# Landmark sums, spreads, squares and loads placed differently in a Nyström attention + MLP kernel

## The chip, the cores and the metric

The kernel runs on one core of a Trainium2 chip. The metric is the device time of one execution in microseconds (us). A core has five engines that run side by side, each with its own queue in program order: TensorE (PE in the profile; its weight loads are listed as PEld), VectorE (DVE), ScalarE (ACT), GpSimd (POOL) and SyncE (SP), whose queue issues all of this kernel's DMAs. Engines wait for each other through semaphores. An engine that waits holds up everything behind it in its queue.

## The reference

q, k and v have 8 batches, 8 heads, 576 rows and 64 columns. The first half is Nyström attention with 32 landmarks; each landmark is the mean of 18 neighbouring rows of q or of k. The second half is a layer norm and an MLP with 2048 hidden units, with a residual:

```
q_lm = q.reshape(B, H, 32, 18, D).mean(axis=3);  k_lm likewise
A, Bm, C = softmax(q k_lm^T), softmax(q_lm k_lm^T), softmax(q_lm k^T)    # each scaled by 1/8
Z = Bm^T / (norm1(Bm) * norminf(Bm));  6 times: Z = 2 Z - Z Bm Z
x = A Z C v                                # (8, 576, 512)
out = x + relu(layernorm(x) * g @ w1) @ w2 # w1 512x2048, w2 2048x512
```

All matmuls run in fp16 with fp32 sums; inputs and output are fp32.

## The kernel before

**The MLP is the bulk of the work.** The 4608 rows of x make 36 blocks of 128 rows; four blocks are a group, so there are nine groups. The generator `mlp` (L825) yields after nearly every matmul of 512 columns. For a group it makes 64 `psh` matmuls (hidden units, evicted by ScalarE into `hT` with a Relu after every fourth) and 64 `pso` matmuls (output; 16 for a block, then one VectorE instruction `ot` that scales with `rstd` and adds x, and two stores). `fill(n)` (L897) takes n steps of this generator, so that n matmuls are put between two pieces of the attention. All order on TensorE, VectorE, ScalarE and GpSimd is that of the program, since every call goes through `keep_in_program_order`.

**Batches 0 and 1** are handled by `attention` (L314) and written out by hand up to L990. **Batches 2 to 7** are handled in sets: set 0 is batch 2, set 1 is batches 3 and 4, set 2 is batches 5 and 6, set 3 is batch 7. A batch has two units of four heads.

**A set is prepared** by a `Coming` object (L508), in three kinds of steps:

- a load (L540): 576 KB of q, k or v into a staging tile `stg`, of which there are six. Loads, stores and DMA transposes all go through SP's queue.
- a cast (L547) by GpSimd, to the fp16 tile `nat` for q or k (eight tiles), to `natv` for v. For a q whose unit number in the set is at least `first_by_pool`, GpSimd also adds up rows in four tensor_tensor instructions, the tiles `asum`, `asum`, `asum` and `s16` (named s in the profile). I call these a q's sums.
- a job: `turn` (L575) is a VectorE transpose of `nat` into `xT`; where GpSimd has made the sums, it also transposes them (`sT`) and adds two halves into `part`, which I call "sT and add". `add_up` (L589) is the other way to `part`: two VectorE tensor_reduce instructions. `spread` (L599) is two TensorE matmuls `psl` on the finished `part` of two units and a copy `lm` from PSUM, after which the scores can be taken.

The jobs of two units stand in the order turn k, add_up k, turn k, add_up k, turn q (add_up q), turn q (add_up q), spread; in a set of four units the first spread comes after the third k pair of jobs and the second at the end.

**A set's attention** is the generator `attention2` (L656). Its steps are: scores of k for each pair of units (`psb`, `psec`, exps on ScalarE, transposes `ecT` on VectorE); the gram and the product with v (`psse`, `pscv`); six iterations (`psn` on TensorE, `st` on VectorE) with the scores of q (`psea`, `ea`) in the first ones; `zc` (`pszc`, then `zcbd` on VectorE); and five row steps per batch (L478: two `psy` matmuls, a reciprocal and `xblk` on VectorE). A set of one batch has 14 steps, a set of two has 21. After each step come some fills, then `settle`, then perhaps a square, then `prepare` for the set after (one cast with its loads, and a job).

**A finished block** calls `block_done` (L742). From group 2 on, GpSimd makes `negm` (minus the mean) and `xn`, SP issues the DMA transpose `xnT`, and ScalarE squares the deviations (`junk`); every fourth block, `deviations` gives `rstd`. `settle` (L738) puts out what is in the list `later`; `a_square` (L978) puts out one item of the list `squares`.

**PSUM**: `psh`, `pso`, `psl` and the transposes `psxt` share three buffers (pool psM); the scores, `pscv` and `psy` share two (ps2).

Of the kernel before, what the change touches and what calls it, by code (L numbers as in the profile page):

```python
# [9 lines left out]
FP16 = mybir.dt.float16  # L10
# [6 lines left out]
P = 128  # L17
# [3 lines left out]
def kernel(  # L21
# [12 lines left out]
    B, H, S, D = q.shape  # L34
# [4 lines left out]
    LM = 32  # L39
# [12 lines left out]
        name=nc.get_next_instruction_name(), act_func_set_id=6, ins=[], outs=[]))  # L52
# [16 lines left out]
    dve, pool, scalar = Ordered(nc.vector), Ordered(nc.gpsimd), Ordered(nc.scalar)  # L69
    act = scalar.activation  # L70

    def MM(o, l, r, rb=0, cb=0, start=True, stop=True, skip=False):
        keep(nc.tensor.matmul(o, l, r, start=start, stop=stop, tile_position=(rb, cb),  # L73
                              skip_group_check=(skip or cb != 0)))
# [88 lines left out]
    for half in range(2):  # L163
        for e in range(2):
            sl = ds(64 * e + 32 * half, 32)
            nc.gpsimd.tensor_copy(
                out=spread16[sl, half, e, :, :],
                in_=ident16[sl, sl][:, None, :].broadcast_to([LM, 2, LM]))
# [23 lines left out]
    for u in range(U):  # L192
        for nm in ("q", "k"):
            cast_qk(0, u, nm, dve)
        if u == 0:

            dve.tensor_copy(out=bones[:], in_=mask4[:, :, None].broadcast_to([P, 4, 32]))
            for i, t in enumerate(zcbd_buf):
                dve.tensor_copy(out=t[:, ds(0 if i % 2 == 0 else 4 * D, 4)],
                                in_=(mask4[:] if i < 2 else heads_of[i % 2]))  # L200
# [43 lines left out]
    asm = ctx.enter_context(tc.tile_pool(name="asm", bufs=2))  # L244
# [263 lines left out]
    class Coming:  # L508
# [38 lines left out]
        def cast(self, i):  # L547
            nm, w = self.parts[i]
            b, u = self.units[w]
            stg = self.stg.pop(i)  # L550
            if nm == "v":
                natv_of[b] = natv_buf[b % NV]
                pool.tensor_copy(
                    out=natv_of[b][:, u, :, :, 0:D].rearrange("p j r d -> p r j d"), in_=stg[:])
                return
            t = nat.tile([P, 2, NJ, D], FP16, name="nat", tag="nat")
            pool.tensor_copy(out=t[:], in_=stg[:])
            self.n16[i] = t
            if nm == "q" and w >= self.first_by_pool:
                s = asum.tile([P, 2, 4, D], FP32, name="asum", tag="asum")  # L560
                s16 = asm.tile([P, 2, D], FP16, name="s16", tag="s16")
                self.sums[i] = s16
                for o, x, y in ((s[:], t[:, :, 0:4, :], t[:, :, 4:8, :]),
                                (s[:, :, 0:2, :], s[:, :, 0:2, :], s[:, :, 2:4, :]),
                                (s[:, :, 0, :], s[:, :, 0, :], s[:, :, 1, :]),
                                (s16[:], s[:, :, 0, :], t[:, :, 8, :])):
                    with nc.allow_low_precision("sums are rounded once, to fp16"):
                        pool.tensor_tensor(out=o, in0=x, in1=y, op=ALU.add)
# [6 lines left out]
        def turn(self, i):  # L575
            nm, w = self.parts[i]
            t = aprep.tile([P, 2, NJ, LM, 2], FP16, name="xT", tag="xT" + nm, bufs=5 if nm == "q" else 4)
            dve.transpose(t[:].rearrange("p r j t x -> p (r j t x)").bitcast(UINT32),
                          self.n16.pop(i)[:].rearrange("p r j d -> p (r j d)").bitcast(UINT32))
            self.xT[nm, w] = t  # L580
            if i in self.sums:
                s = asm.tile([P, 2, LM // 2, 2, 2], FP16, name="sT", tag="sT")
                dve.transpose(s[:].rearrange("p r l a x -> p (r l a x)").bitcast(UINT32),
                              self.sums.pop(i)[:].rearrange("p r d -> p (r d)").bitcast(UINT32))
                dve.tensor_tensor(out=self.part_of(nm, w), in0=s[:, :, :, 0, :], in1=s[:, :, :, 1, :],
                                  op=ALU.add)
# [12 lines left out]
        def spread(self, y):  # L599
            part = self.part.pop(y)  # L600
            psl = psM.tile([P, 2, 8, LM], FP32, name="psl", tag="pm")
            for half in range(2):
                MM(psl[:, half, :, :].rearrange("p k c -> p (k c)"),
                   spread16[:, half, :, :, :].rearrange("p e a w -> p (e a w)"),
                   part[:].rearrange("p n w r l x -> p (n w r l x)"))
            lm = asm.tile([P, 8, 2, LM], FP16, name="lm", tag="lm", bufs=3)
            dve.tensor_copy(out=lm[:].rearrange("p k h c -> p h k c"), in_=psl[:])
            for i, nm in enumerate(("q", "k")):
                for x in range(2):
                    self.lm[nm, 2 * y + x] = lm[:, ds(4 * i + 2 * x, 2), :, :].rearrange(  # L610
                        "p r h (l x) -> p r (h l) x", x=2)
# [124 lines left out]
    later, squares, negms = [], [], {}  # L736

    def settle():  # L738
        while later:
            later.pop(0)()  # L740

    def block_done(j):  # L742
        g, u = divmod(j, 4)
        if g == 0:
            mean_of(j, dve)
            center(j, scalar if u % 2 == 0 else dve)
        elif g == 1:
            mean_of(j, dve)
            later.append(lambda: center(j, scalar))
        else:  # L750
            later.append(lambda: mean_of(j, pool))
            later.append(lambda: center(j, pool) if g <= mlp_at[0] + 1
                         else uncentered.setdefault(g, []).append(j))
        (squares if g <= 1 else later).append(lambda: square(j))
        if u == 3:
            if g == 1:
                later.append(lambda: ln_ready.add(1))
            (squares if g <= 1 else later).append(lambda: deviations(g))

    def mean_of(j, engine):  # L760
        negms[j] = mstat.tile([P, 1], FP32, name="negm", tag="negm", bufs=16)
        engine.tensor_scalar(out=negms[j][:], in0=rowsum.pop(j)[:], scalar1=-1.0 / DM,
                             scalar2=0.0, op0=ALU.mult, op1=ALU.add)
# [18 lines left out]
    def square(j):  # L782
        g, u = divmod(j, 4)
        if u == 0:
            variances[g] = mstat.tile([P, 4], FP32, name="var", tag="var")
        junk = mxn.tile([P, DM], FP16, name="junk", tag="junk", bufs=1)
        act(junk[:], x_blk[j][:], AF.Square, bias=negms[j][:],
            accum_out=variances[g][:, u:u + 1])

    def deviations(g):  # L790
        lnv = mstat.tile([P, 4], FP32, name="lnv", tag="lnv")
        act(lnv[:], variances.pop(g)[:], AF.Ln, bias=eps_ln[:], scale=1.0 / DM)
        rstds[g] = mstat.tile([P, 4], FP32, name="rstd", tag="rstd")
        act(rstds[g][:], lnv[:], AF.Exp, scale=-0.5)
        ln_ready.add(g)
# [101 lines left out]
    def fill(n):  # L897
        for _ in range(n):
            if not next(stream, False):
                return  # L900
# [56 lines left out]
    cast_v(1)  # L957
    fetch_w2()

    sets = [Coming((2,), 1), Coming((3, 4), 2), Coming((5, 6)), Coming((7,))]  # L960

    def prepare(c, casts, jobs):
        for _ in range(casts):
            if c.casts:
                c.next_cast()
                if not c.loads and c is not sets[-1]:
                    sets[sets.index(c) + 1].next_load()
                else:
                    c.next_load()
        for _ in range(jobs):  # L970
            c.next_job()

# [5 lines left out]
    def a_square():  # L978
        if squares:
            squares.pop(0)()  # L980

    n = 0
    for what in a1:
        fill(fills[what])
        settle()
        if what in ("iteration", "product"):
            a_square()
        if what in ("product", "zc", "rows"):
            n += 1
            prepare(sets[0], 1, 1 if n > 3 else 0)  # L990
    for _ in range(2):
        prepare(sets[0], 1, 1)
        fill(6)

    counts = [[9, 20] + 6 * [6] + [7] + 4 * [7] + [10]]
    counts += [[8, 12, 18, 18, 10, 10, 8, 8, 8, 8, 8] + 10 * [7]]
    counts += [[12, 14, 20, 20, 12, 12, 12, 10, 10, 10, 10] + 10 * [10]]
    counts += [[15, 18] + 6 * [12] + [12] + 5 * [12]]
    for c, after, count in zip(sets, sets[1:] + [None], counts):
        while c.jobs:  # L1000
            prepare(c, 1, 1)
            fill(3)
        for step, _ in enumerate(attention2(c.bs, c)):
            fill(count[step])
            settle()
            if step >= 2:
                a_square()
            if after:
                prepare(after, 1, 1)
    for _ in stream:  # L1010
        pass

# [29 lines left out]
```

## Time and profile before

| | |
|---|---|
| median of five runs | 329.97 us (329.29 to 331.67) |
| profiled execution, its own time | 329.8 us |
| its span, first to last instruction | 328.1 us |
| granted TensorE clock, mean | 0.995 of full speed |
| TensorE, weight loads | 310.9 us, 156.1 us |
| VectorE, ScalarE, GpSimd busy | 151.8, 151.1, 121.6 us |
| moved by DMA | 50.32 MB, 153 GB/s on average |

How to read the lines that follow. The page gives each engine's busy time, then the span in 40 slices of 8.2 us with a digit for tenths of busy time (9 is 90% or more); PEclk is the clock granted to TensorE in tenths. A line of waits says which engine waited, for whom, and the total, the count and the longest in us. A line of the timeline has the start in us, the duration, the engine, the line of the helper (L67 and L73 are the helpers that keep the order), the operation, the tiles as out<-in, and the shapes; in square brackets stands idle time in front of it and what ended that. A line of a tile's statistics has the count and the least, the median and the largest duration in ns.

### The profile page before, as it was taken

The page shows a single profiled execution, that of the slowest core. Times are in us where ns is not written, and L with a number is a line of the kernel's source. Part 1 is how long each engine was busy: PE and PEld are TensorE (multiplying, and loading weights), DVE is VectorE, ACT ScalarE, POOL GpSimd, SP SyncE. Part 2 cuts the span into 40 slices and gives each one's busy share as a digit, 9 for nine tenths or more (in the row PEclk, how much of TensorE's full clock was granted, in tenths as well). Part 3 has the DMA queues.
Part 4 walks back from the last instruction along what each step waited for, and adds up shares of the span by engine and source line. Part 5 has one row for each costly group of instructions (what it writes and reads, how often), then busy time and mean ns, then how long its engine had stood idle before and what let it go on. Part 6 is the DMA issues. An engine that isn't in the chain of part 4 may idle for free.

```text
span 328.1 us, 7899 instructions
## 1 busy us (share of the span) xinstructions
PE 310.9 (95%) x3248; PEld 156.1 (48%) x3248; DVE 151.8 (46%) x398; ACT 151.1 (46%) x295; POOL 121.6 (37%) x186
## 2 busy tenths in 40 slices
PE   7889999599989999989999999999999999999994
PEld 6568654244534444434544444444444444444443
DVE  3666249868987556955455345431243110010012
ACT  3376843349532670469322573663058216305600
POOL 4489777864799280449700020500011200000000
PEclk9999999799999999999999999999999999999999
DMA  7999999958997795870023012420241124032023
GB/s 274 394 387 388 386 388 233 388 146 254 319 253 247 200 271 155 252 133 21 2 66 81 21 32 64 82 50 2 64 108 23 32 66 94 2 78 51 2 56 72
DMA packets 38700, 50.32 MB, mean 153 GB/s; under 512 B 17540, under 2 KB 17800, under 8 KB 38664
## 3 DMA queue, kind: packets, MB, share of 16 engines
q1 hardware_dynamic: 38664, 49.82, 52.7%
q8 instruction: 25, 0.41, 0.5%
q14 instruction: 11, 0.09, 0.1%
HBM read 36.70 MB, written 9.44 MB: 141 GB/s over the span
## 4 chain that ended last, share of the span: by engine, by line
PE 82%; DVE 12%; DMA 3%; issue 1%; SPq 0%; DVEq 0%
PE psh L73 39%; PE pso L73 31%; DVE part L67 3%; DVE xblk L67 2%; DMA stg<-in_k_dram 2%; PE psn L73 2%; PE psy L73 2%; DVE xT L67 2%; PE pscv L73 2%; DVE ot L67 1%; PE psec L73 1%; DMA xnT<-xn 1%; PE pst L77 1%; PE psea L73 1%; DVE rcpd L67 1%
## 5 line engine op out<-in xcount | busy, mean ns | idle before, releaser
L73 PE MATMUL psh<-xnT,w 128*128 128x512 f16 (+1 forms) x640 | 135.2, 358 | 1.2 <-DMA xnT<-xn 1.2
L73 PE MATMUL pso<-w,hT 128*128 128x512 f16 (+1 forms) x592 | 133.9, 375 | 0.7 <-issue 0.7
L67 ACT ACTIVATE hT<-psh 128x512 f16<-128x512 f32 x144 | 84.9, 599 | 89.1 <-PE psh L73 88.8
L73 PEld LDWEIGHTS <-w 128*128 128x128 f16 x640 | 59.1, 98 | 59.0 <-issue 2.9
L73 PEld LDWEIGHTS <-hT 128*128 128x128 f16 x592 | 56.3, 98 | 59.8 <-issue 3.2
L67 DVE SCALAR_TENSOR_TENSOR ot<-pso,rstd,xblk 128x512 f32<-128x512 f32 (+1 forms) x37 | 27.2, 734 | 76.5 <-PE pso L73 76.3
L67 POOL TENSOR_SCALAR negm<-rowsum 128x1 f32<-128x1 f32 x28 | 5.4, 191 | 97.2 <-DVE xblk L67 93.7
L67 ACT ACTIVATE junk<-xblk,negm 128x512 f16<-128x512 f32 x36 | 26.0, 723 | 25.7 <-POOL negm L67 25.6
L67 POOL CAST nat<-stg 128x1152 f16<-128x1152 f32 x28 | 31.8, 1146 | 12.7 <-DMA stg<-in_q_dram 9.9
L67 DVE SCALAR_TENSOR_TENSOR xblk<-psy,rcpd 128x512 f32<-128x512 f32 (+1 forms) x40 | 27.6, 691 | 2.2
L67 DVE SCALAR_TENSOR_TENSOR st<-st,psn 128x128 f16<-128x128 f16 (+2 forms) x36 | 11.4, 317 | 33.5 <-PE psn L73 33.4
L67 POOL CAST natv<-stg 128x1152 f16<-128x1152 f32 x16 | 18.5, 1162 | 7.8 <-DMA stg<-in_v_dram 7.8
L67 DVE TENSOR_REDUCE part<-xT 128x32 f16<-128x576 f16 x30 | 21.0, 743 | 0.0
L67 POOL TENSOR_SCALAR xn<-xblk,negm 128x512 f16<-128x512 f32 x28 | 19.3, 694 | 4.8 <-DMA xnT<-xn 3.7
L67 DVE RECIPROCAL rcpd<-psy 128x8 f32<-128x8 f32 (+1 forms) x40 | 8.1, 203 | 24.0 <-PE psy L73 23.8
L67 DVE STREAM_TRANSPOSE xT<-nat 128x576 uint32<-128x576 uint32 x24 | 18.4, 766 | 0.0
L73 PE MATMUL psy<-zcbd,ea 128*128 128x260 f16 (+1 forms) x80 | 15.7, 276 | 0.9 <-DVE zcbd L67 0.8
L73 PEld LDWEIGHTS <-st 32*32 32x32 f16 x448 | 5.7, 89 | 15.1 <-issue 10.4
L73 PEld LDWEIGHTS <-ea 128*128 128x128 f16 (+1 forms) x80 | 7.3, 100 | 10.4 <-issue 2.2
L67 ACT ACTIVATE ea<-psea 128x576 f16<-128x576 f32 x12 | 7.2, 649 | 10.7 <-PE psea L73 10.7
L67 ACT ACTIVATE ec<-psec 128x576 f16<-128x576 f32 x12 | 8.9, 815 | 6.8 <-PE psec L73 6.8
L67 POOL TENSOR_TENSOR asum<-asum 128x256 f32<-128x256 f32 (+1 forms) x18 | 10.7, 593 | 1.4
(101 smaller groups left out, 208.1 us busy)
## 6 DMA issues: line engine op xcount, KB each, us to landing
stg<-in_q_dram SPq DMA_DIRECT2D x16, 576.0 KB, 7.5
stg<-in_k_dram SPq DMA_DIRECT2D x16, 576.0 KB, 7.9
out_dram<-ot SPq DMA_DIRECT2D x70, 128.0 KB, 2.3
wstg<-in_moe_w_ch_dram SPq DMA_DIRECT2D x16, 512.0 KB, 6.9
stg<-in_v_dram SPq DMA_DIRECT2D x10, 576.0 KB, 7.3
stg<-in_v_dram SPq DMA_DIRECT2D x12, 288.0 KB, 8.6
xnT<-xn SPq DMA_TRANSPOSE x28, 2.5
out_dram<-ot SPq DMA_DIRECT2D x4, 64.0 KB, 1.9
```

Source lines behind the costliest of these rows:

```text
L67: return lambda *args, **kw: keep(getattr(self.engine, op)(*args, **kw))
L73: keep(nc.tensor.matmul(o, l, r, start=start, stop=stop, tile_position=(rb, cb), skip_group_check=(skip or cb != 0)))
L77: keep(nc.tensor.matmul(o, i_, idn, is_transpose=True, tile_position=(0, 0)))
```

## The change

It changes where work stands and who does it, and no matmul:

- `first_by_pool` becomes 0 for set 0 (was 1) and 1 for set 1 (was 2): one more q in each has its sums made by GpSimd, and VectorE does sT and add for it instead of add_up. `s16` gets four buffers (was two), `sT` one (was two).
- The copy `lm` of the six spreads goes from VectorE to ScalarE.
- Squares and deviations of all groups go to the list `squares`; one item is put out per step, from step 0 of a set.
- `prepare` casts a q or k only while fewer than eight `nat` tiles wait for their turn, and after a cast it issues loads until three staged tiles wait for their casts, over all sets (before: one load per cast, so six).
- Each step of a set has its own number of fills and says whether it carries a job. Jobs that are left when a set begins are followed by 8 fills each (5 in set 1; before: 3). Set 0's spread has 16 more fills ahead of it.

```diff
-                s16 = asm.tile([P, 2, D], FP16, name="s16", tag="s16")
+                s16 = asm.tile([P, 2, D], FP16, name="s16", tag="s16", bufs=4)
...
-                s = asm.tile([P, 2, LM // 2, 2, 2], FP16, name="sT", tag="sT")
+                s = asm.tile([P, 2, LM // 2, 2, 2], FP16, name="sT", tag="sT", bufs=1)
...
-            dve.tensor_copy(out=lm[:].rearrange("p k h c -> p h k c"), in_=psl[:])
+            scalar.copy(lm[:].rearrange("p k h c -> p h k c"), psl[:])
...
-        (squares if g <= 1 else later).append(lambda: square(j))
+        squares.append(lambda: square(j))
         if u == 3:
             if g == 1:
                 later.append(lambda: ln_ready.add(1))
-            (squares if g <= 1 else later).append(lambda: deviations(g))
+            squares.append(lambda: deviations(g))
...
-    sets = [Coming((2,), 1), Coming((3, 4), 2), Coming((5, 6)), Coming((7,))]
+    sets = [Coming((2,)), Coming((3, 4), 1), Coming((5, 6)), Coming((7,))]
...
-            if c.casts:
+            if c.casts and (c.parts[c.casts[0]][0] == "v" or len(c.n16) < 8):
                 c.next_cast()
-                if not c.loads and c is not sets[-1]:
-                    sets[sets.index(c) + 1].next_load()
-                else:
-                    c.next_load()
+                while sum(len(x.stg) for x in sets) < (3):
+                    left = [x for x in sets if x.loads]
+                    if not left:
+                        break
+                    left[0].next_load()
...
-    for _ in range(2):
+    while len(sets[0].jobs) > 1:
         prepare(sets[0], 1, 1)
         fill(6)
-
-    counts = [[9, 20] + 6 * [6] + [7] + 4 * [7] + [10]]
-    counts += [[8, 12, 18, 18, 10, 10, 8, 8, 8, 8, 8] + 10 * [7]]
-    counts += [[12, 14, 20, 20, 12, 12, 12, 10, 10, 10, 10] + 10 * [10]]
-    counts += [[15, 18] + 6 * [12] + [12] + 5 * [12]]
-    for c, after, count in zip(sets, sets[1:] + [None], counts):
+    fill(16)
+
+    steps = [[(10, 0), (12, 1)] + 6 * [(6, 1)] + [(8, 1)] + 5 * [(6, 0)]]
+    steps += [[(6, 0), (8, 0), (12, 0), (12, 0), (6, 0), (6, 0), (5, 0), (5, 0), (5, 0), (5, 0), (8, 0)] + 3 * [(6, 0)] + 7 * [(7, 1)]]
+    steps += [[(12, 0), (14, 1), (16, 1), (16, 1)] + 6 * [(9, 1)] + [(10, 1)] + 10 * [(8, 1)]]
+    steps += [[(15, 0), (18, 0)] + 6 * [(12, 0)] + [(12, 0)] + 5 * [(12, 0)]]
+    for c, after, plan in zip(sets, sets[1:] + [None], steps):
         while c.jobs:
             prepare(c, 1, 1)
-            fill(3)
-        for step, _ in enumerate(attention2(c.bs, c)):
-            fill(count[step])
+            fill(5 if c is sets[1] else 8)
+        for (count, jobs), _ in zip(plan, attention2(c.bs, c)):
+            fill(count)
             settle()
-            if step >= 2:
-                a_square()
+            a_square()
             if after:
-                prepare(after, 1, 1)
+                prepare(after, 1, jobs)
+    settle()
+    while squares:
+        a_square()
     for _ in stream:
         pass
```

## The prediction

> **What bounds the kernel now.** I read the page first: engine sums, then the 40 slices.
>
> ```profile
> PE 310.9 (95%) x3248; PEld 156.1 (48%) x3248; DVE 151.8 (46%) x398; ACT 151.1 (46%) x295; POOL 121.6 (37%) x186
> PE   7889999599989999989999999999999999999994
> PEclk9999999799999999999999999999999999999999
> ```
>
> TensorE is busy 95% of 328.1 us; no other engine reaches half. The change removes no matmul, so only TensorE's idle time, and a lower clock, can be won. Slice 7 (57 to 66 us) has the one deep hole and the one clock drop. Next, who made TensorE wait (total, times, longest):
>
> ```profile
> PE psl L73 <- DVE part L67: 6.4, 3, 4.3
> PE psh L73 <- DMA xnT<-xn: 1.2, 1, 1.2
> PE psy L73 <- DVE zcbd L67: 0.8, 2, 0.5
> ```
>
> psl is the spread matmul of a set; it needs VectorE's last landmark sum. The timeline gives its three waits: 4.27 us at 61.44, 1.40 at 95.38, 0.73 at 135.69. psh waited 1.24 us at 142.08 for a DMA transpose. One of the two zcbd waits, 0.26 us at 129.28, lies where the change acts. The hole in windows (span, busy by engine, clock, DMA):
>
> ```profile
> 56.80:61.40 4.60, 0.37 (x2) 0.10 (x1) 4.52 (x9) 1.29 (x3) 4.31 (x7) 1.00 1.05 394
> 61.40:62.60 1.20, 1.16 (x5) 0.39 (x4) 0.74 (x2) 0.00 (x0) 1.07 (x1) 0.82 1.05 396
> 62.60:63.80 1.20, 1.20 (x50) 0.61 (x49) 1.13 (x4) 0.21 (x1) 1.03 (x1) 0.50 1.05 404
> 63.80:65.20 1.40, 1.40 (x15) 0.84 (x8) 0.78 (x3) 1.29 (x2) 0.42 (x2) 0.50 1.06 374
> 65.20:66.90 1.70, 1.70 (x24) 0.68 (x21) 1.18 (x3) 0.68 (x2) 1.41 (x2) 0.89 0.93 293
> ```
>
> VectorE is busy 4.52 of 4.60 us while TensorE stands; then TensorE runs at half clock. Lost to the clock: 0.18 x 1.2 + 0.50 x 1.2 + 0.50 x 1.4 + 0.11 x 1.7 = 1.7 us. VectorE's timeline shows what it worked on:
>
> ```profile
> 57.46 0.77 DVE L67 STREAM_TRANSPOSE xT<-nat 128x576 uint32<-128x576 uint32 x1
> 58.26 1.41 DVE L67 TENSOR_REDUCE part<-xT 128x32 f16<-128x576 f16 x2
> 59.59 0.77 DVE L67 STREAM_TRANSPOSE xT<-nat 128x576 uint32<-128x576 uint32 x1
> 60.28 0.20 DVE L67 STREAM_TRANSPOSE sT<-s 128x64 uint32<-128x64 uint32 x1
> 60.52 0.87 DVE L67 TENSOR_TENSOR part<-sT 128x64 f16<-128x64 f16 x1
> 61.86 0.69 DVE L67 CAST lm<-psl 128x512 f16<-128x512 f32 x1 [0.47 <-PE psl L73]
> ```
>
> From start to start: turn 0.70, add_up 1.33, sT 0.24, an ot 0.66 (56.80 to 57.46), a row with its reciprocal 0.85 (133.00 to 133.85). A 512-column matmul takes 0.216 (13.81 us for 64 in the chain), a psy pair, a psl pair or a block's four psxt 0.22 each.
>
> **Part by part.** *Set 0's spread.* Ahead of psl the change puts 28 fills instead of 18: nine pso and one psxt more, 9 x 0.216 + 0.22 = 2.16 us. TensorE was there at 61.44 - 4.27 = 57.17, now at 59.3. On VectorE q of unit 0 loses add_up (1.33) and gains sT and add (0.43). From 57.46: turn, sT, add, turn, sT, add = 2.26, so 59.7. But ot2, now ahead of psl, may own the PSUM buffer that psl takes (three serve pso, psh, psxt and psl): + 0.66. And the add:
>
> ```profile
> L67 DVE TENSOR_TENSOR part<-sT x9: 192/193/868, 60.5 to 174.1; 128x64 f16<-128x64 f16 x9
> ```
>
> The 868 ns one began at 60.52 and ended at 61.39, as GpSimd's cast of 60.20 to 61.34 ended. The Trainium skill, "SBUF — State Buffer", section on the two sides of the memory, speaks against the change here: a VectorE operation with two SBUF inputs and a GpSimd operation lock each other out for a whole instruction. The change makes two more such adds, and two more runs of GpSimd sums beside them. By the row's median an add costs 0.19; by the rule up to the rest of a GpSimd instruction (a cast or first sum, 1.15). The trace has both, so 0.19 to 0.87 each. Ready: 59.7 to 61.7. I take one locked add and the ot, 61.0: the wait falls from 4.27 to 1.7 (0.4 to 2.4). Gain 2.6.
>
> *The clock.* A wait of 1.40 us at 95.38 cost no clock, one of 4.27 did. By these rows alone a wait of 1.7 could go either way: 0 to 1.7 us. The skill's "TensorE: Matmul & The Clock Gate", Part 1, puts the fall to half rate after about 3.4 us of idleness; 1.7 is well under. I take the whole 1.7. After psl, eight fills instead of three cover lm (psb waited about 0.3): gain 0.3.
>
> *lm on ScalarE.* The six casts cost VectorE 685 ns each. The nearest ScalarE row, a copy of 512 columns from PSUM (xnT), takes 581. It queues behind squares (0.72 + 0.19), each of which waits for GpSimd's negm, and hT evictions queue behind it. At every spread 1.1 us or more of fills stand between; cost 0, and 0.6 where that cover is gone.
>
> *Set 1's spread* (wait 1.40). Only eight of its 15 jobs go into set 0's steps, none into the rows; seven follow with five fills each. From the last psy of set 0: VectorE ends its row at 1.4, then two add_ups, two ot, three turns, two sT and adds = 2.66 + 1.32 + 2.10 + 0.86 = 6.9, so 8.3; TensorE has 6 + 30 fills, psy and psl, 7.8 + 0.44 = 8.2. Wait 0.1, with both adds locked 1.5; I take 0.5. Gain 0.9.
>
> *Set 2.* zcbd has no job ahead of it: gain 0.26. The second spread leaves the rows for the seven jobs behind them, with 48 fills (10.4 us) for some 6 us of VectorE work: gain 0.73. The last seven rows are the price: rows 7 x 0.85, jobs 7.0 and two ot 1.3 make 14.3 us of VectorE, against TensorE's 7 x (7 x 0.216 + 0.22) = 12.1. It falls 2.2 behind; psy waits only for the row two before, which allows 2 x 1.73 - 1.4 = 2.1. Cost 0 to 1.5; I take 0.
>
> *psh of group 3* (wait 1.24). Between xn of block 15 and its first use stood 19 fills and three rows, 4.8 us; now 30 fills and five, 7.6. Gain 1.24.
>
> *Fewer fills in set 1's attention.* Step 0 has 6 fills (1.3 us) before psec of the second pair, which needs two ec evictions (0.74 start to start, 0.23 after psec): wait 0.45. The gram then waits for the exp behind them and the softmax: 0.45. The second psea after 6 fills waits for two ea (0.65 each): 0.2. An iteration (psn, st 0.42) fits in 5 fills. Cost 1.1, between 0 and 2.
>
> *Squares and negm.* One list item per step, in ScalarE's order. A square may come one step later; its cover is that step's fills, and no group's rstd is wanted within 3 us. Cost 0.
>
> *GpSimd and the load queue.* Two more q sums, 1.157 + 0.730 + 0.457 + 0.427 = 2.77 us each. Four s16 buffers cover a GpSimd that runs ahead. SP is in order:
>
> ```profile
> 70.07 1.11 SPq L802 DMA_DIRECT2D out_dram<-ot  x2
> 71.28 2.29 SPq L780 DMA_TRANSPOSE xnT<-xn  x1
> 73.66 0.52 SPq L82 DMA_DIRECT2D stg<-in_q_dram  x1
> ```
>
> ```profile
> 77.89 1.14 POOL L67 CAST nat<-stg 128x1152 f16<-128x1152 f32 x1 [4.52 <-DMA stg<-in_q_dram]
> ```
>
> The load behind ot3's store and xnT of block 8 was issued 4.4 us after ot3 (69.29) and used at 77.89. With three loads ahead instead of six, that place falls to unit (3,1)'s q, three casts earlier. ot3 will be near 64.4, so its cast starts near 73 and its sums end near 76.9. VectorE wants them at step 7, near 77.6: margin 0.7, and behind that turn stand st, zcbd and the rows. From there GpSimd has two k casts, two q with sums (3.95 each), three v casts and three negm and xn (2.06 a pair): xn of block 11 at 93.2, landing at 95.7 with the median 2.5 us. TensorE starts group 2's psh near 95.6. In the trace that transpose took 7.4 (issued 90.57) among the loads; now at most three are ahead. Cost 0 to 5; I take 0.5, near the median.
>
> **The sum.** Gains 2.6 + 1.7 + 0.3 + 0.9 + 0.26 + 0.73 + 1.24 = 7.7; costs 1.1 + 0.5 = 1.6; net 6.1. The profiled execution took 329.8 us with a span of 328.1, the median is 329.97: they differ by less than the sum's error. Forecast 329.97 - 6.1 = 323.9.
>
> **Rivals.** *All waits go.* 4.27 + 1.7 + 0.3 + 1.40 + 0.26 + 0.73 + 1.24 = 9.9 and no cost: 320.1. For it: TensorE's 95%; against it: the short fills of set 1.
> *The lock eats the relief.* The adds in sets 0 and 1 and in set 2's rows all wait for GpSimd: 0.7 + 1.0 + 1.5 more, 327.1. For it: three of nine adds were lengthened in the trace; against it: six were not.
> *The change doesn't shorten the queue.* The transpose of block 11 takes 7.4 again: group 2 waits 5.0 instead of 0.5, and the clock falls once (1.7): 323.9 + 4.5 + 1.7 = 330.1, no change.
> *Slower: GpSimd late in set 0.* If two loads, not one, are held for 4.5 us, q of (3,1) is 9 us late against a margin of 0.7: VectorE stops in step 7, st and zcbd with it, TensorE stands 8.3 us and the clock falls: 323.9 + 8.3 + 1.7 = 333.9. It decides from about 6 us of lateness. For it: GpSimd waited 4.52 once; against it: between stores and xnT there is one such place in the set.
>
> **Chances.** A measurement can tell about 0.5%, 1.65 us: no change is 328.3 to 331.6. Forecast (321.8 to 326) 0.50, all waits go 0.17, lock 0.15, queue 0.10, slower 0.08. So faster 0.82, same 0.10, slower 0.08. The range 319.7 to 329.5 leaves out the slower case, half of the queue's and a little at the lower end.
>
> **What would show it.** Right: psl's waits total 2 to 3 us with none over 3.4, slice 7 of the clock at 9, no psh wait at group 3, VectorE's CAST lm gone and six ScalarE copies instead. Wrong: a psh wait for xnT at group 2, VectorE waiting for GpSimd's s or nat in set 0's iterations, psy waiting for xblk in set 1's rows, or lm waiting behind a square.

## The result, and the profile after

The changed kernel takes 329.37 us (median of 43 runs, 327.48 to 334.09), the kernel before 330.16 in the same comparisons (80 runs, 328.27 to 331.88). The ratio is 0.9974, 95% interval 0.9962 to 0.9987: 0.8 us faster where the forecast was 6.1. Medians and ranges here and below are of all executions, while the ratios leave out the few that are over 1.5% above the fastest of their kernel. The profiled execution took 329.3 us with a span of 327.6 and a mean granted clock of 0.993.

The page's engine sums and slices:

```profile
PE 311.5 (95%) x3248; PEld 156.8 (48%) x3248; DVE 146.3 (45%) x392; ACT 154.2 (47%) x301; POOL 126.9 (39%) x194
PE   8789999999976969999999999999999999999994
PEclk9999999999997999999999999999999999999999
```

The work moved as planned: VectorE lost 5.5 us, ScalarE gained 3.1, GpSimd 5.3. The hole and the clock drop of slice 7 are gone. But there are new holes in slices 11, 12 and 14, and the clock drops in slice 12 (98 to 106 us). TensorE's waits (total, times, longest) say for whom:

```profile
PE psh L73 <- DMA xnT<-xn: 2.8, 1, 2.8
PE psn L73 <- issue: 2.6, 1, 2.6
PE psl L73 <- ACT lm L67: 1.8, 1, 1.8
...
PE psl L73 <- DVE part L67: 0.6, 1, 0.6
PE psy L73 <- DVE zcbd L67: 0.5, 1, 0.5
```

psl's 6.4 us of waiting for VectorE shrank to 0.6. Three waits that were not in the profile before stand above it: group 2's psh for the transpose of block 11, set 1's psl for the copy lm (now ScalarE's), and a pause of TensorE that no engine and no data DMA released ("issue").

The timeline shows how the first spread got its gain, on VectorE and TensorE (start, duration; idle time before in brackets):

```profile
57.56 0.77 DVE L67 STREAM_TRANSPOSE xT<-nat 128x576 uint32<-128x576 uint32 x1
58.25 0.20 DVE L67 STREAM_TRANSPOSE sT<-s 128x64 uint32<-128x64 uint32 x1
58.49 0.44 DVE L67 TENSOR_TENSOR part<-sT 128x64 f16<-128x64 f16 x1
...
59.78 0.26 DVE L67 TENSOR_TENSOR part<-sT 128x64 f16<-128x64 f16 x1
...
60.09 0.39 PE L73 MATMUL psl<-part,spread 128*128 128x256 f16 x2 [0.64 <-DVE part L67]
```

The tensor_reduce pair of 1.41 us has gone from between the turns, and psl starts at 60.09 instead of 61.44.

And it shows how the loss of set 1 came about. The lines are of SP's queue, GpSimd, ScalarE and TensorE, in order of time:

```profile
57.67 9.08 SPq L802 DMA_DIRECT2D out_dram<-ot  x6
66.85 2.02 SPq L780 DMA_TRANSPOSE xnT<-xn  x1
68.92 0.56 SPq L82 DMA_DIRECT2D stg<-in_q_dram  x1
...
73.42 1.15 POOL L67 CAST nat<-stg 128x1152 f16<-128x1152 f32 x1 [9.14 <-DMA stg<-in_q_dram]
...
91.55 0.57 SPq L82 DMA_DIRECT2D stg<-in_k_dram  x1
...
93.56 0.57 SPq L82 DMA_DIRECT2D stg<-in_k_dram  x1
...
93.65 0.70 POOL L67 TENSOR_SCALAR xn<-xblk,negm 128x512 f16<-128x512 f32 x1
...
94.23 1.18 SPq L802 DMA_DIRECT2D out_dram<-ot  x2
...
95.42 0.19 POOL L67 TENSOR_SCALAR negm<-rowsum 128x1 f32<-128x1 f32 x1
95.50 1.33 SPq L780 DMA_TRANSPOSE xnT<-xn  x1
95.65 0.72 ACT L67 ACTIVATE junk<-xblk,negm 128x512 f16<-128x512 f32 x1 [0.67 <-POOL negm L67]
...
96.37 0.56 ACT L67 CAST lm<-psl 128x512 f16<-128x512 f32 x1
...
96.98 0.38 PE L73 MATMUL psl<-part,spread 128*128 128x256 f16 x2 [1.85 <-ACT lm L67]
...
100.81 0.59 PE L73 MATMUL psh<-xnT,w 128*128 128x512 f16 x2 [2.80 <-DMA xnT<-xn]
```

The load of unit (3,1)'s q (68.92) stands in SP's queue behind stores (57.67) and the transpose of block 8 (66.85); GpSimd stood still 9.14 us for it. From there to 97.5 us GpSimd works without a gap in which it could win this back, and two things hang on it. First, xn of block 11 ends at 94.35; SP issues its transpose at 95.50, after the store of 94.23, and psh starts 5.3 us after that. Second, ScalarE has in its queue the square of block 12, which waits for GpSimd's negm, and behind it the copy lm of one spread, whose PSUM the next psl has to have. The windows that follow (span, busy time of PE, PEld, DVE, ACT, POOL, granted clock, DMA share, GB/s) show the price:

```profile
96.50:100.80 4.30, 1.03 (x5) 0.48 (x5) 0.75 (x1) 1.02 (x2) 2.14 (x2) 1.00 1.07 234
100.80:103.00 2.20, 2.19 (x52) 0.92 (x52) 0.00 (x0) 0.36 (x1) 0.00 (x0) 0.61 0.99 373
103.00:106.00 3.00, 3.00 (x56) 1.15 (x55) 1.06 (x3) 2.48 (x6) 2.37 (x3) 0.71 1.17 229
```

TensorE worked 1.03 of 4.30 us, and then lost 0.39 x 2.2 + 0.29 x 3.0 = 1.7 us to the lower clock: as much as the change had won back in set 0.

**The balance.** Won against the profile before: set 0's psl 4.27 - 0.64 = 3.6, its clock 1.7, set 2's psl 0.73, group 3's psh 1.24, one zcbd wait 0.26; 7.5. Lost: set 1's psl 1.85 - 1.40 = 0.45, psh of group 2 2.8, the clock 1.7, the pause 2.60 - 0.75 = 1.85; 6.8. Net 0.7. The two profiled executions differ by 0.5 (329.8 and 329.3), the medians by 0.8.

### The profile page after: what moved, and what is told of

It is laid out like the page before. It is cut to its first block, busy times and chain, and to the rows that moved or that the text cites. A ratio compares the mean times of both kernels' runs of the same rounds, so it can differ in the third digit from the quotient of the medians.

```text
span 327.6 us, 7900 instructions
## 1 busy us (share of the span) xinstructions
PE 311.5 (95%) x3248; PEld 156.8 (48%) x3248; DVE 146.3 (45%) x392; ACT 154.2 (47%) x301; POOL 126.9 (39%) x194
## 4 chain that ended last, share of the span: by engine, by line
PE 77%; POOL 6%; DVE 6%; DMA 5%; issue 2%; ACT 1%; SPq 1%; POOLq 0%
PE psh L73 35%; PE pso L73 31%; PE psy L73 2%; DMA stg<-in_k_dram 2%; POOL asum L67 2%; PE psn L73 2%; DMA xnT<-xn 2%; PE pscv L73 2%; DVE xblk L67 2%; POOL nat L67 1%; POOL natv L67 1%; DMA stg<-in_q_dram 1%; PE psec L73 1%; DVE part L67 1%; DVE ot L67 1%
## 5 line engine op out<-in xcount | busy, mean ns | idle before, releaser
L67 DVE TENSOR_REDUCE part<-xT 128x32 f16<-128x576 f16 x26 | 18.3, 745 | 0.1
L67 POOL TENSOR_TENSOR asum<-asum 128x256 f32<-128x256 f32 (+1 forms) x22 | 13.0, 592 | 1.7
L67 POOL TENSOR_TENSOR asum<-nat 128x512 f32<-128x512 f16 x11 | 12.7, 1155 | 0.9
L73 PE MATMUL psn<-st 32*32 32x64 f16 (+1 forms) x384 | 9.3, 189 | 3.1 <-issue 2.6
```

The costliest lines, as they stand in the source:

```text
L67: return lambda *args, **kw: keep(getattr(self.engine, op)(*args, **kw))
```

## The experiments

Theory (load order): with three staged tiles instead of six, the one place in SP's queue behind ot3's stores and the transpose of block 8 falls to a load that is wanted three casts earlier. All of GpSimd's work up to set 1's attention is late by what it waits there, and that lateness eats the gain. Rivals: GpSimd simply has too much to do (two more q sums); lm is in the wrong queue on ScalarE; the pause, or the load rule as such, is what counts. Each ratio is against runs of the kernel before on the same chip (medians of 330.1 to 330.4 us).

**limit6: the load rule alone taken back.**

```diff
-                while sum(len(x.stg) for x in sets) < (3):
+                while sum(len(x.stg) for x in sets) < (6):
```

> The changed kernel with up to six staged tiles instead of three. Theory (load order): the load of q of unit (3,1) no longer stands behind the store of ot3, so GpSimd's 9.1 us wait for it goes; xn of block 11 ends near 88.5 instead of 94.3, lm0 of set 1 isn't held, psl's wait for it (1.85) and group 2's psh wait (2.80) go, and with them the clock drop (1.7): about 323. Rival 1 (too much GpSimd work): the two further q sums keep GpSimd late, 327 to 329. Rival 2 (lm on ScalarE is what holds TensorE): the 1.85 stays, 327.5.

Measured 326.25 us (324.86 to 327.71), ratio 0.9873 (0.9843 to 0.9904). In this kernel's waits of TensorE neither xnT nor lm is left:

```profile
PE psn L73 <- issue: 2.9, 2, 2.2
PE psl L73 <- DVE part L67: 1.3, 2, 0.7
```

xn of block 11 starts at 87.68 there instead of 93.65. It is the earlier start that removes the wait, not a faster transpose: issued at 90.1, the transpose of block 11 took 6.4 us to land, longer than the 5.3 in the changed kernel. Still, 326.25 is not the "about 323" that the theory expected.

The forecast had 5.3 us more than the change gave; 3.3 of them ((0.9974 - 0.9873) x 330) come from this one number. The longer pause, 2.23 us at 118.48, is followed by windows at a clock of 0.72, 0.50 and 0.93 over 2 us each: 0.28 x 2 + 0.50 x 2 + 0.07 x 2 = 1.7 us more, about half of what is missing from the 323.

**sums_dve: the sums of the two q back on VectorE, three staged tiles kept.**

```diff
-    sets = [Coming((2,)), Coming((3, 4), 1), Coming((5, 6)), Coming((7,))]
+    sets = [Coming((2,), 1), Coming((3, 4), 2), Coming((5, 6)), Coming((7,))]
```

> The changed kernel with first_by_pool back at 1 and 2: q of (2,0) and of (3,1) are added up by VectorE again. Load-order theory: GpSimd still stands some 9 us for the load; only the one sum behind the load counts, so xn of block 11 ends 2.8 earlier, psl's wait for lm goes and group 2's wait falls under 0.5; VectorE's additional work makes the first psl wait 1.5 instead of 0.64: about 325. Rival 1 (too much GpSimd work): xn of block 11 ends 5.5 earlier and the time is 323.5. Rival 2: lm's wait stays, 327.5.

Measured 326.95 us (325.84 to 332.69), ratio 0.9901 (0.9865 to 0.9938); the profiled execution, 329.6 us, is at the slow end of that. GpSimd waits about as long as in the changed kernel (8.79 us in front of the cast at 72.45), but with less work behind it, psh waits 1.94 us at 97.75 instead of 2.80, and psl no longer waits for lm. Neither the theory's 325 nor the rival's 323.5 was met; the trace has a pause of 3.2 us with a clock drop behind it. Taken alone this run would speak for the rival; limit6_sums_dve, below, decides.

**lm_dve: the copy lm back on VectorE, three staged tiles kept.**

```diff
-            scalar.copy(lm[:].rearrange("p k h c -> p h k c"), psl[:])
+            dve.tensor_copy(out=lm[:].rearrange("p k h c -> p h k c"), in_=psl[:])
```

> The changed kernel with the copy lm on VectorE again. Load-order theory: psl's wait for lm goes, but the same lateness then falls on group 2's psh, whose wait grows from 2.8 to about 4.6: no change, 329.4. Rival 2 (lm on ScalarE is what holds TensorE): 327.5 or less. VectorE's 0.69 in front of the second psl of set 1 costs at most 0.7.

Measured 329.13 us (327.56 to 334.98), ratio 0.9959 (0.9935 to 0.9984): not to be told from the changed kernel. The wait of psl for lm is gone, and TensorE waits for the transpose that much longer:

```profile
PE psh L73 <- DMA xnT<-xn: 3.8, 1, 3.8
```

So lm on ScalarE is where the lateness shows first, not where it comes from. In this chain the wait is handed on: ScalarE's square waits for GpSimd, lm stands behind the square, TensorE waits for lm or, without it, for the transpose.

**before_limit3: the load rule alone, in the kernel before.** Only the new rule of `prepare`, with the limit 3 and the condition on waiting casts, is put into it.

> The kernel before with the limit of three staged tiles alone (and with its condition on waiting casts). Load-order theory: the load of q of (3,1) and those behind it wait for the store of ot2 and ot3, GpSimd stands longer, and VectorE waits for casts in set 0: slower by 1 to 4, 331 to 334. Rival 1 (the sums, not the loads): no change, 329.5 to 330.7. A gain would come only from group 3's transpose, whose wait of 1.24 may go.

Measured 334.55 us (333.58 to 338.07), ratio 1.0143 (1.0105 to 1.0181). The rule costs 1.4% there; taken out of the changed kernel, in limit6, it brings 1.0% (0.9873 against 0.9974). The size is at the upper end of what the theory gave, but its way was another: psl's waits for VectorE fell (6.4 to 4.6 us in all). GpSimd waited 27.7 us for loads of q and k instead of 12.7, a square on ScalarE waited 5.0 us for GpSimd's negm, the eviction `hT` stood behind that square, and TensorE waited for `hT`:

```profile
PE pso L73 <- ACT hT L67: 2.3, 1, 2.3
```

Right after it the clock was at half for 3.4 us, a second time in this trace: 2.3 + 1.7 = 4.0 of the 4.7 us lost. It is the same chain as with lm, GpSimd late and ScalarE held by a square, at another place.

**limit6_wide: limit6 with seven fills instead of five in four iterations of set 1**, to see whether the pause comes from too many short instructions in a row.

```diff
-    ... (6, 0), (6, 0), (5, 0), (5, 0), (5, 0), (5, 0), (8, 0)] ...
+    ... (6, 0), (6, 0), (7, 0), (7, 0), (7, 0), (7, 0), (8, 0)] ...
```

> Six staged tiles as in limit6 (326.25), and seven fills instead of five in set 1's iterations 2 to 5. In limit6 TensorE stands 2.2 us in the middle of psn with nothing to wait for, until 1.5 us after a 16 KB packet of the instruction queue; 25 such packets make the program of TensorE. Theory (instructions late): few fills between many small matmuls use instructions up faster than they are fetched; eight more fills are 1.7 us, so the wait falls to about 0.5 and the clock drop of some 1.3 behind it goes: 323 to 324. Rival (the pause has nothing to do with the rate of instructions): 326.3. Group 3's psh comes eight fills earlier, which may cost up to 0.5.

Measured 327.24 us (326.12 to 332.56), ratio 0.9885 (0.9845 to 0.9926). The pause only went from 2.2 to 1.9 us, and psh of group 3, which eight fills brought forward, now waits 2.0 for its transpose. The density of instructions in these iterations doesn't explain the pause.

**limit63: six staged tiles for the loads of sets 0 and 1, three for those of sets 2 and 3.**

```diff
-                while sum(len(x.stg) for x in sets) < (3):
+                while True:
                     left = [x for x in sets if x.loads]
-                    if not left:
+                    if not left or sum(len(x.stg) for x in sets) >= (6 if left[0] in sets[:2] else 3):
```

> Limit of six staged tiles for the loads of sets 0 and 1, of three for those of sets 2 and 3. Load-order theory: set 0 is as in limit6, group 2's transposes meet fewer loads: 325.5 to 326.5. Rival (the rule of three is bad everywhere, as it puts loads behind stores in set 1 too): 328 or more. The instruction theory expects the pause of 2 us in set 1's iterations to stay, since up to six loads still run there at once.

Measured 323.73 us (322.88 to 325.36), ratio 0.9804 (0.9767 to 0.984): 6.4 us faster than the kernel before, just clear of limit6's interval, and faster than the 325.5 to 326.5 expected. Its timeline at the places shown above:

```profile
74.99 1.15 POOL L67 CAST nat<-stg 128x1152 f16<-128x1152 f32 x1 [4.81 <-DMA stg<-in_q_dram]
...
88.86 0.69 POOL L67 TENSOR_SCALAR xn<-xblk,negm 128x512 f16<-128x512 f32 x1
...
97.60 0.39 PE L73 MATMUL psl<-part,spread 128*128 128x256 f16 x2 [0.80 <-DVE part L67]
...
98.47 0.59 PE L73 MATMUL psh<-xnT,w 128*128 128x512 f16 x2
```

GpSimd still waits, 4.81 us, but for a later unit's q, when it is further on in its list: xn of block 11 starts at 88.86 instead of 93.65, 4.8 us earlier, and psh of group 2 doesn't wait. Against limit6 the trace is better by the pause and the clock (2.9 - 2.0 + 1.7 = 2.6 us) and worse by longer waits of psl, psn and psxt (1.3); the two spans differ by 1.5. That the clock didn't fall here is partly chance of where the pause lay, as the last section shows: limit6's two executions with a mean clock of 0.998 took 324.86 and 325.20 us, limit63's four with 0.998 or more took 322.88 to 324.97.

**slots3: limit63, and three of the six staging tiles withheld from set 2's first load on**, so that at most three of its loads can be in flight (three one-element GpSimd writes and a late read of them are added).

```diff
+                    while left[0] not in sets[:2] and len(held) < 3:
+                        held.append(stage.tile([P, 2, NJ, D], FP32, name="held", tag="stg"))
+                        pool.memset(held[-1][:, 0, 0, 0:1], 0.0)
```

> As limit63, with three of the six staging tiles held back from the first load of set 2 on, so that no more than three loads of set 2 are in the DMA queue at a time (three small memsets and three small copies on GpSimd are added). Instruction theory with the loads as the cause: a 16 KB packet then waits behind at most three loads instead of six, the pause falls from 2.2 to under 1 us: 323.5 to 325. Rival (the rate of instructions alone sets it): the pause stays, 326. If GpSimd then waits for loads in set 1, its rows pay: 327 or more.

Measured 325.83 us (323.06 to 326.96), ratio 0.9839 (0.9791 to 0.9887). TensorE's list of waits has no pause at all; at its head stands psh of group 3:

```profile
PE psh L73 <- DMA xnT<-xn: 2.1, 1, 2.1
```

So with fewer loads in flight the pause is gone, in the one trace that there is. But it saved nothing: without it TensorE reaches group 3's psh 3.3 us earlier than in limit63 (133.7 instead of 137.0), while the transpose of block 15 is issued only 0.5 earlier (131.79 instead of 132.30). It waits there instead, and after that wait the clock falls. The time is above the 325 expected; the interval overlaps with limit63's, and the two executions with a clock of 0.999 or more took 323.06 and 323.69.

**limit6_sums_dve: limit6 with the sums on VectorE**, the edits of both.

> limit6 with first_by_pool back at 1 and 2. Load-order theory: with the load in time GpSimd has room for the two further sums and VectorE loses 0.9 in set 0 and 0.9 in set 1: the first psl waits 1.5, the second 1.4, against 0.7 and 0.6 in limit6: 327.8. Rival (GpSimd's work or the lock between it and VectorE eats what VectorE gains): the same as limit6, 326.3, or less.

Measured 328.83 us (326.15 to 332.32), ratio 0.9929 (0.9901 to 0.9956). With loads in time, taking the sums away from GpSimd makes the kernel about 2 us slower than limit6 (0.9873), whose interval it just touches (its profiled execution, 326.7, is at the fast end of its runs). The rival "too much GpSimd work" would have it at least as fast; the runs speak against it. With the sums on VectorE the load rule makes no difference that can be told (0.9901 and 0.9929, intervals overlapping); with them on GpSimd it decides between 326.25 and 329.37. That GpSimd has the slack to take the wait in the one case and not in the other is the likely reason; it is argued, not shown, since psh waits 1.94 us in sums_dve too.

**limit4: four staged tiles instead of three.**

```diff
-                while sum(len(x.stg) for x in sets) < (3):
+                while sum(len(x.stg) for x in sets) < (4):
```

> The changed kernel with four staged tiles instead of three. If the place of one load behind ot3's store and the transpose of block 8 is what costs, the late load falls to a later cast, which is wanted later: GpSimd's longest wait for a q falls from 9.1 to some 4 to 7 us, the waits of psl for lm and of psh of group 2 for xnT are under 2 us together, time 326 to 328. If three or four make no difference because loads in general crowd the queue, it stays at 329 to 329.6.

Measured 326.4 us (324.74 to 327.85), ratio 0.9869 (0.9835 to 0.9903): one more tile is as good as three more. GpSimd's waits (total, times, longest) show that the late load is now another one:

```profile
POOL nat L67 <- DMA stg<-in_k_dram: 8.2, 8, 4.7
POOL nat L67 <- DMA stg<-in_q_dram: 4.7, 6, 1.4
```

It is a k, not a q: the place in SP's queue moved on by casts, as the theory said, and the wait is half of 9.14. psh waits 0.9 us in all for xnT, and psl not at all for lm. Between three, four and six, what counted was not the number of loads but which load stands in that place.

**before_limit63: limit63's load rule alone, in the kernel before.**

> The kernel before, with the load rule of the fastest kernel so far (six staged tiles for the loads of sets 0 and 1, three for those of sets 2 and 3) and nothing else of the change. If the load rule only lets the placement of fills, jobs and sums pay, it brings little by itself: 328.5 to 330.5, with psl still waiting for VectorE about 6 us in all. If the 6.4 us by which that kernel beats the one before come from its loads and the placement is worth nothing, this gives 324 to 325.

Measured 330.14 us (329.12 to 333.08), ratio 0.9993 (0.9975 to 1.0011); psl waits 6.1 us for VectorE (in the profiled execution, the slowest of the 22, at 333.08). A good load rule alone is worth nothing. The 2% of limit63 need the placement of fills, jobs, sums and copies, which pays once loads come in time.

**limit63_lm_dve: limit63 with lm on VectorE.**

> The fastest kernel so far (323.7) with the copy lm of the spreads on VectorE again, as before. With GpSimd in time no square holds lm up on ScalarE, and the prediction put lm on ScalarE at a cost of nothing. On VectorE each copy of 0.69 us stands ahead of turns, ot and st; fills cover most of that: 323.5 to 325. If moving lm is a gain of its own, 325.5 or more; if it is a loss even with loads in time, under 323.

Measured 326.48 us (324.02 to 327.59), ratio 0.9853 (0.9812 to 0.9894). This is above the 325 that "worth nothing" allowed; but its interval overlaps with limit63's, and in the profile the difference is the pause, 2.2 us here, with a clock drop behind it in slice 14. The mean clocks on record say that this is most of it: the two executions at 0.997 and 0.999 took 324.02 and 324.05 us, like limit63, and the four at 0.982 to 0.995 took 326.47 to 327.59. That lm gains anything of its own on ScalarE is not shown.

**limit63_fill22: limit63 with 22 instead of 16 fills ahead of set 0's spread.**

> The fastest kernel so far (323.7) with 22 instead of 16 fills ahead of set 0's spread, 6 x 0.216 = 1.3 us more, against the 1.09 us for which psl waits there for VectorE's last add. If the fills cover that wait and are not missed later: 322.6 to 323.2. If the fills are missed where they are taken from (a later psh finds its xnT on the way, as with three staging tiles held back), 323.7 to 326.

Measured 323.76 us (322.0 to 325.09), ratio 0.9794 (0.9755 to 0.9833): the same as limit63. psl no longer waits for VectorE's add there, and psh waits 1.0 us for xnT, which it hadn't: the fills are missed where they were taken from. limit63 and this one are the fastest kernels here, faster than the kernels before and after.

## Why the prediction was right and wrong

Right, each with what it measured:

- *Set 0's spread and the clock.* Forecast wait 1.7 with 0.4 to 2.4 open; measured 0.64. Forecast that 1.7 us of clock come back; slice 7 is at 9. The reason given, that 1.7 is well under 3.4, doesn't hold: waits of 2.15 us cost a clock drop here, and 1.7 was close to that. The ot that was feared ahead of psl came after both adds (at 59.95). The adds took 0.44 and 0.26 against the median of 0.19 before. GpSimd was casting v meanwhile (57.73 to 59.99), in instructions of 1.13, so neither add waited for a whole one; what lengthened them is not shown.
- *Set 2's spread, psh of group 3, zcbd.* All three waits are gone: 0.73 + 1.24 + 0.26.
- *GpSimd's times.* Cast of (3,1)'s q near 73, measured 73.42; sums' end 76.9, measured 77.66; xn of block 11 done at 93.2, measured 94.35. GpSimd's queue had been read rightly, to about 1 us. Which load would be late had been named too.

Wrong:

- *"Cost 0 to 5; I take 0.5", of GpSimd and the load queue.* This is the step that failed: the late load was foreseen, and its cost to group 2's transpose and psh was put at 0.5 us. The landing was forecast for 95.7; psh found its input at 100.81. Of these 5.1 us, xn was 1.15 late, the transpose was issued 1.15 us after xn's end, since the store of 94.23 stood in front of it on SP, and it took 5.3 us instead of the median of 2.5. TensorE, itself held up by lm, waited 2.8 of them, and the clock fell for 1.7. The cost was 4.5, inside the bounds, at the far end. The median was of all transposes; the row nearest to it was the same block's 7.4 us, which the prediction quoted and set aside because "at most three are ahead". Two loads of 576 KB were issued in the 4 us before it (91.55, 93.56); at the 387 GB/s of the full slices, two are an estimated 3.0 us of queue by themselves. The third rival, with 5.0 us and one clock drop, had the slow transpose right, though not GpSimd's lateness, and came out 0.7 us from the result; it was given one chance in ten.
- *"lm on ScalarE ... cost 0".* Its condition was that fills cover each square's wait for negm. With GpSimd 9.14 us late, the square of block 12 stood before lm and psl waited 1.85, where at most 0.6 had been allowed. With limit6 or limit63 this wait doesn't occur, so the term was sound as long as GpSimd is in time, and it was the same failed step that broke it.
- *Set 1's spread.* Forecast 0.5, measured 1.85 for that reason; with loads in time 0.59 in limit6 and 0.80 in limit63.
- *The pause.* 2.60 us against 0.75 before was not in the sum at all; it is in none of the prediction's rows. Mending the load rule doesn't remove it (2.23 in limit6, 1.96 in limit63).
- *"Fewer fills in set 1's attention", cost 1.1.* TensorE's waits show no psec, gram or psea wait that is new. The term was too large; what it ought to have been can't be read off, since the late psh changes where those steps fall.

Together: 4.0 us more for the failed step, 1.35 for set 1's spread behind it and 1.85 for the pause, against 1.0 that set 0's spread won beyond its forecast and 1.1 of short fills that didn't come. That is 5.1 of the 5.3 us by which the forecast missed.

The forecast of 323.9 us is what limit63 measures, 323.73, with the load rule mended. That is partly chance, since it contains the pause and lacks the cost of the short fills. What is shown is that the change without its load rule is worth about 6 us once the loads come in time (limit63 at 0.9804, before_limit63 at 0.9993).

## What to carry to other kernels

When a change alters how many loads may be ahead, write out the in-order DMA queue and look which load comes to stand behind the stores and transposes: here a wait of 4.8 us at one cast cost psh nothing (limit63), and one of 9.1 us three casts earlier cost 4.5. When an engine gets more work and its inputs later in one change, cost its last product with the queue as full as the trace shows it for that very transfer, not with a median over quiet times. Test a limit by its neighbours: 3, 4 and 6 staged tiles gave 329.4, 326.4 and 326.25.

## What the runs showed of the hardware

**TensorE stops for its own code.** The page lists a DMA queue of kind "instruction" with 25 packets, 0.41 MB, 16 KB each. In four traces of this case the pause ends shortly after such a packet:

```
kernel    packet starts, took    TensorE goes on    pause
before    101.54, 1.03 us        104.07             0.75
after     120.02, 1.31 us        122.86             2.60
limit6    115.86, 1.08 us        118.48             2.23
limit63   115.77, 1.31 us        118.57             1.96
```

That the packets are TensorE's instructions follows from counting. The page has 3248 matmuls and 3248 weight loads, 260 for each packet. Counted by the trace's records of TensorE from its start, the pause comes after TensorE's 2753rd instruction in the kernel before, after the 3265th in the three others of the table, after the 3009th and the 3265th in sums_dve and limit6_sums_dve, and after the 4033rd in before_limit3 and before_limit63: always a multiple of 256 apart. It ends 1.3 to 1.6 us after the packet's end.

Why the packet is late is shown only in part. Data packets keep the DMA engines busy then (share 1.05 at 119 to 123 us of the changed kernel). In limit63 the packet starts 0.65 us before TensorE gets to that instruction (115.77, 116.42); in slots3, with set 2's loads kept to three, it starts 3.8 us ahead (111.29, 115.12) and there is no pause. That the packet waits behind data packets is argued from this.

**The clock falls on a grid of 3.41 us.** The Trainium skill, "TensorE: Matmul & The Clock Gate", Part 1, puts the fall to half rate after about 3.4 us of idleness. Here shorter gaps were enough, and the traces show when. Each drop inside the span lasts 3.41 us (one in before_limit63 twice that, 6.83), and each stretch at full clock between the first rise and a drop is a whole multiple of 3.413 us: 58.03 in the kernel before (17), 95.57 after (28), 112.64 in limit6 (33). So the clock changes only at the marks of a grid with that step; the marks lie elsewhere in each trace. With the span cut at them:

```
kernel           between two marks   TensorE idle   clock after
before             58.74 to  62.16       2.70          half
after              97.89 to 101.30       2.80          half
after             118.37 to 121.78       1.52          full
after             121.78 to 125.19       1.08          full
limit6            115.46 to 118.88       2.23          half
limit63           114.80 to 118.21       1.60          full
slots3            133.05 to 136.47       2.15          half
sums_dve           95.10 to  98.51       1.94          full
before_limit63    156.40 to 159.82       1.80          half
```

In all fourteen traces a drop followed every stretch between two marks with 2.15 us of idleness or more and none with less than 1.80; between these, one of five. The pause of 2.60 us in the changed kernel cost no clock because a mark fell into it. A drop costs 0.5 x 3.41 = 1.7 us, or 0.005 of an execution's mean clock. So whether a wait of 2 to 3 us costs 1.7 us more depends on where it lies on the grid. The mean clocks above are read that way; that the marks also shift between executions of one kernel is inferred, since of each kernel one execution was traced.
